# Token-first layout for the turned blocks of u: one 2 KB run per row of each partition-to-partition move

## The chip, the cores and the metric

The kernel runs on one core of a Trainium2 chip. The metric is the device time of one execution in microseconds (us), lower is better. Before the change it is 1478.62 us, the median of 3 runs that lie between 1475.41 and 1482.45.

## The reference

The input `x` has 8 batches of 3136 tokens with 256 features. An FNet mixing (the real part of an FFT over the tokens and over the features) is followed, row by row, by a SoLU block with a layer norm between its two products:

```python
X = np.fft.fft(np.fft.fft(x, axis=1), axis=2).real   # 8 x 3136 x 256
x = X.reshape(25088, 256)
h = x @ w_in                                          # 1024 features
e = np.exp(h - max(h)); sm = e / (sum(e) + 1e-9)
solu = h * sm
ln = (solu - mean(solu)) / sqrt(var(solu) + 1e-6) * g_ln
out = ln @ w_out                                      # 25088 x 256
```

All of it is fp32.

## The kernel before, in words

The batches are taken in 4 pairs. The FFT over 3136 = 49 x 64 tokens is done in two steps: `transform1` works on the 49 and writes its result to DRAM (`zd`), `turn` (L156) reads it back with other axes on the partitions (4 DMAs, L160), and `transform2` (L163) does the 64. The FFT over features is folded into the weights `Wi`. By symmetry one pair needs 25 values of the index `k1`; a **unit** is one pair at one `k1`, so there are 100 units. A unit gives two tiles of 128 tokens by 1024 features, sign 0 and sign 1 (a row and its mirror image); the four units with `k1` = 0 have sign 0 alone.

Within a unit the work goes over the engines like this. TensorE forms the even and the odd half of h (`up`, L195, into two PSUM buffers). VectorE takes the even half (`even`, L201), joins the halves into h for each sign and finds the maximum (`join`, L209, L214). ScalarE takes the exponential (`expo`, L220). VectorE multiplies it by h (`product`, L228), which gives u. ScalarE squares u for the variance (L237), while VectorE turns the same u in blocks of 32 x 32 (`turn_blocks`, L258, and L260 for a unit with one sign). For the second product the features must lie on the partitions. The blocks are turned, but each still sits in the wrong group of 32 partitions, so `move_blocks` (L262) sends each of the 4 x 4 pairs of partition groups to its place with one DMA (L269): 16 DMAs of 64 KB for each unit, all issued by the SP queue. TensorE then multiplies (`down`, L275): 8 chunks of 128 features, with the turned u as the stationary operand (the one that LDWEIGHTS loads) and `Wo` as the moving one. Each fp32 product is two LDWEIGHTS and two MATMUL in the profile, so a unit has 32 of these. `store` (L278) scales the result on ScalarE (L281); sign 0 leaves by two DMAs of SP (L289), sign 1 by an indirect DMA of GpSimd (L284).

The order of the work is written out by hand (L421 to L452), and each engine and queue goes through its own instructions in that order. In the iteration of unit i, TensorE does `up` of i, `transform2` of unit i+1, a piece of `transform1` for the next pair (16 of the 25 iterations, in three of the four pairs), and `down` of unit i-2. SP gets, in order: a store of `transform1` (L154, every second piece) or at one place in each pair the four DMAs of `turn`, then the two stores of unit i-2, the 16 moves of unit i, and a load of the next pair's input (L96). So a unit's turned blocks have somewhat under two iterations to arrive. VectorE also folds the next pair's input (L109 to L111), in 8 of the 25 iterations. Tile `v` has 2 buffers, `uT` 3, the PSUM pool that `down` writes to 4.

Before the change the tile `v` holds, in each partition, feature first and sign innermost: element (f, s) is at 2f + s. A 32 x 32 block is 32 neighbouring f, and a move takes, from each of 32 partitions, 8 separate runs (one for each chunk of 128 features) of 64 numbers, 256 bytes. `uT` holds chunk first, then token and sign, so `down` reads its stationary operand with a step of 2 numbers, 8 bytes.

Of the kernel before, what the change touches and what calls it, by code (L numbers as in the profile page):

```python
# [8 lines left out]
FP32 = mybir.dt.float32  # L9
# [6 lines left out]
P = 128  # L16
# [15 lines left out]
def kernel(  # L32
# [19 lines left out]
    nc = tc.nc  # L52
    B, S, D = x.shape
    FF = moe_w_in.shape[1]
    KF = FF // P
# [21 lines left out]
    Wo = const.tile([P, KF, D], FP32, name="Wo")  # L77
# [29 lines left out]
    def fold_features(o, i):  # L107
        up, down = i[:, :, 1:128], i[:, :, 255:128:-1]
        nc.vector.tensor_tensor(out=o[:, :, 1:128], in0=up, in1=down, op=ALU.add)  # L109
        nc.vector.tensor_tensor(out=o[:, :, 129:256], in0=up, in1=down, op=ALU.subtract)  # L110
        nc.vector.tensor_copy(out=o[:, :, 0:129:128], in_=i[:, :, 0:129:128])  # L111
# [141 lines left out]

    def turn_blocks(t, s):

        if s == 0:
            t.v = fpool.tile([P, FF, 2], FP32, tag="v", name="v32", bufs=2)
        nc.vector.transpose(out=t.v[:, :, s], in_=t.u[s])  # L258
        if len(t.signs) == 1:
            nc.vector.transpose(out=t.v[:, :, 1], in_=t.u[s])  # L260

    def move_blocks(t):  # L262

        t.uT = fpool.tile([P, KF, 4, 64], FP32, tag="uT", name="uT", bufs=3)
        v = t.v.rearrange("p (c q n) s -> p q c (n s)", q=4, n=32)
        for i in range(4):
            for q in range(4):
                a, b = slice(32 * i, 32 * i + 32), slice(32 * q, 32 * q + 32)
                nc.sync.dma_start(out=t.uT[b, :, i, :], in_=v[a, q])  # L269

    def down(t, s):
        uT = t.uT.rearrange("p c i (n s) -> p c (i n) s", s=2)
        ps = ps_m.tile([P, D], FP32, tag="m", name="ps_o")
        for c in range(KF):
            nc.tensor.matmul(ps, uT[:, c, :, s], Wo[:, c, :], start=(c == 0), stop=(c == KF - 1))  # L275
        return ps

    def store(t, s, ps):  # L278
# [124 lines left out]
    with tc.manual_schedule():  # L403
# [13 lines left out]
        fpool = ctx.enter_context(tc.tile_pool(name="fpool", bufs=2))  # L417
# [3 lines left out]
        for i in range(len(units) + 2):  # L421
# [14 lines left out]
            if old:  # L436
                ps_o = [down(old, s) for s in old.signs]
            if cur:
                for s in cur.signs:
                    product(cur, s)  # L440
                for s in cur.signs:
                    square(cur, s)
                    turn_blocks(cur, s)
            if old:
                store(old, 0, ps_o[0])
            if cur:
                move_blocks(cur)
                stats(cur)
# [80 lines left out]
```

## Time and profile before

| | |
|---|---|
| median of 3 runs | 1478.62 us |
| the profiled execution's own time | 1484.27 us |
| its span (first to last instruction) | 1482.5 us |
| mean granted TensorE clock | 0.936 |
| matmul busy | 1223.0 us (82%) |
| VectorE busy | 961.7 us (65%) |
| ScalarE busy | 613.8 us (41%) |
| GpSimd busy | 471.9 us (32%) |
| bytes moved by DMA | 189.66 MB in 486718 packets |

The profile is of one execution. PE is TensorE's matmul, PEld its loading of weights, DVE VectorE, ACT ScalarE, POOL GpSimd, SP the sync engine, which only issues DMAs here; a q behind a name is the engine's instruction queue. A row of the timeline has the start, the duration, the engine, the line, the operation, the tile written and the tiles read, the count, and in brackets the idle time before it and what ended that. A row of a line's instructions has the smallest, median and largest duration in ns and the first and last start in us. A group row has busy time and mean ns. Runs of like instructions are merged into one row of a timeline, so that the difference of two starts gives the pace.

### The profile page before, as it was taken

The numbers are of one execution on the slowest core, as the hardware profiler recorded it, in microseconds if no ns is written. First come the engines' busy times: TensorE is split into PE (matmuls) and PEld (weight loads), VectorE is DVE, ScalarE is ACT, GpSimd is POOL, SyncE is SP. The second block draws the span as 40 slices with busy tenths as digits, with TensorE's granted clock in tenths as the row PEclk, the third lists the DMA queues.
The fourth block names the chain that finished last, engine by engine and source line by source line (L and its number), as shares of the span: only waits on it lengthen the run. The fifth ranks groups of instructions, "written<-read, shape, count | busy, mean of one in ns | idle before, by whom it ended". The sixth has DMA issues, their size and how long they took to land.

```text
span 1482.5 us, 17170 instructions
## 1 busy us (share of the span) xinstructions
PE 1223.0 (82%) x4864; PEld 916.3 (62%) x4864; DVE 961.7 (65%) x1481; ACT 613.8 (41%) x1149; POOL 471.9 (32%) x892
## 2 busy tenths in 40 slices
PE   1633798999959889998959899889968889989996
PEld 1312476667747667676747577657746666767665
DVE  2598766767646676767655676666646666767671
ACT  0101454444534444445434345444524444444441
POOL 3400434343213334434213343333212333333331
PEclk8566999999979999999989999999998999999998
DMA  9540665655574656555574656555574444444443
GB/s 243 178 84 0 139 139 143 149 134 125 124 159 107 139 143 145 134 148 126 118 159 108 146 125 150 139 145 129 116 164 110 108 103 109 109 107 109 108 110 85
DMA packets 486718, 189.66 MB, mean 128 GB/s; under 512 B 446326, under 2 KB 472702, under 8 KB 486368
## 3 DMA queue, kind: packets, MB, share of 16 engines
q1 hardware_dynamic: 471952, 157.61, 48.0%
q0 software_dynamic: 8704, 25.44, 5.9%
q10 hardware_dynamic: 5968, 5.52, 1.7%
q8 instruction: 40, 0.66, 0.2%
q14 instruction: 54, 0.44, 0.1%
HBM read 44.78 MB, written 38.80 MB: 56 GB/s over the span
## 4 chain that ended last, share of the span: by engine, by line
SPq 44%; PE 30%; DMA 13%; DVE 6%; issue 5%; POOL 1%; ACT 1%; POOLq 0%; ACTq 0%; DVEq 0%
SPq L269 39%; PE ps_o L275 19%; PE ps_h L195 9%; SPq L289 4%; DMA uT<-v 4%; DMA g<-zd 3%; DMA xa<-in_x_dram 2%; DMA out_dram<-ot 2%; DVE ex L302 2%; PE ps L169 1%; DMA xb<-in_x_dram,idx 1%; POOL xa L118 1%; PE ps L149 1%; DVE h L209 0%; DVE rest L330 0%
## 5 line engine op out<-in xcount | busy, mean ns | idle before, releaser
L275 PE MATMUL ps_o<-Wo,uT 128*128 128x256 f32 x3136 | 730.7, 393 | 161.9 <-DMA uT<-v 87.2
L275 PEld LDWEIGHTS ps_o<-Wo,uT 128*128 128x128 f32 x3136 | 628.4, 203 | 247.4 <-issue 149.6
L195 PE MATMUL ps_h<-Wi,q 128*128 128x512 f32 x800 | 360.2, 593 | 4.0 <-DVE ev L201 2.5
L228 DVE SCALAR_TENSOR_TENSOR u<-h,u 128x1024 f32<-128x1024 f32 x196 | 232.7, 1224 | 140.6 <-ACT u L220 140.6
L237 ACT ACTIVATE h<-u,nmean 128x1024 f32<-128x1024 f32 x196 | 223.6, 1142 | 229.4 <-POOL nmean L230 229.4
L284 POOL DMA_INDIRECT out_dram<-ot,idx x96 | 114.6, 1194 | 605.1 <-DMA out_dram<-ot 395.2
L220 ACT ACTIVATE u<-h,neg 128x1024 f32<-128x1024 f32 x196 | 223.6, 1141 | 188.0 <-DVE neg L214 186.2
L209 DVE CUSTOM_DVE_ANT_0 h<-ev,ps_h 128x1024 f32<-128x1024 f32 x196 | 231.7, 1219 | 77.9 <-PE ps_h L195 46.9
L201 DVE SCALAR_TENSOR_TENSOR ev<-w_mid,q,ps_h 128x1024 f32<-128x1024 f32 x100 | 127.8, 1278 | 217.6 <-PE ps_h L195 217.3
L195 PEld LDWEIGHTS ps_h<-Wi,q 128*128 128x128 f32 x800 | 151.7, 190 | 152.4 <-issue 145.6
L258 DVE STREAM_TRANSPOSE v<-u 128x1024 f32<-128x1024 f32 x196 | 233.0, 1228 | 0.1
L177 ACT COPY q<-ps 128x257 f32<-128x257 f32 x100 | 37.4, 374 | 253.8 <-PE ps L171 253.7
L230 POOL TENSOR_SCALAR nmean<-usum 128x1 f32<-128x1 f32 x196 | 84.0, 440 | 161.2 <-DVE u L228 159.3
L149 PE MATMUL ps<-y,F 98*100 98x258 f32 (+3 forms) x288 | 80.3, 419 | 41.1 <-DVE y L111 41.0
L281 ACT ACTIVATE ot<-ps_o,rs 128x256 f32<-128x256 f32 x196 | 83.9, 459 | 69.8 <-PE ps_o L275 69.7
L169 PEld LDWEIGHTS ps<-T,g 128*128 128x128 f32 x400 | 60.4, 191 | 47.4 <-issue 47.4
L149 PEld LDWEIGHTS ps<-y,F 98*100 98x100 f32 x288 | 48.0, 191 | 54.7 <-DVE y L111 21.3
L118 POOL TENSOR_TENSOR xa<-xa,xb 98x1020 f32<-98x1020 f32 (+1 forms) x32 | 72.7, 2272 | 27.7 <-DMA xa<-in_x_dram 19.0
L249 POOL TENSOR_SCALAR v<-ssq 128x2 f32<-128x2 f32 (+1 forms) x100 | 25.0, 250 | 169.6 <-ACT h L237 169.6
L252 POOL TENSOR_TENSOR rs<-v,neg_half 128x2 f32<-128x2 f32 (+1 forms) x100 | 72.0, 720 | 7.8
L169 PE MATMUL ps<-T,g 128*128 128x128 f32 x400 | 60.7, 274 | 0.0
L152 ACT COPY z<-ps 100x512 f32<-100x512 f32 x64 | 36.2, 569 | 36.5 <-PE ps L149 27.2
(53 smaller groups left out, 461.0 us busy)
## 6 DMA issues: line engine op xcount, KB each, us to landing
uT<-v SPq DMA_DIRECT2D x1600, 64.0 KB
zd<-z SPq DMA_DIRECT2D x32, 400.0 KB
g<-zd SPq DMA_DIRECT2D x16, 800.0 KB
out_dram<-ot SPq DMA_DIRECT2D x200, 64.0 KB
xa<-in_x_dram SPq DMA_DIRECT2D x32, 392.0 KB
raw_in_moe_w_in_dram<-in_moe_w_in_dram ACTq DMA_DIRECT2D x1, 2048.0 KB
raw_in_moe_w_out_dram<-in_moe_w_out_dram ACTq DMA_DIRECT2D x1, 2048.0 KB
out_dram<-ot,idx POOLq DMA_INDIRECT x96, 2.9
```

Of the source, the lines that this page charges most:

```text
L149: nc.tensor.matmul(o[..., cs], F[:, 2 * t + h, :], i[..., cs], start=first, stop=True, skip_group_check=True)
L169: nc.tensor.matmul(ps[:, h * P : (h + 1) * P], pr.g[:, k1, h * P : (h + 1) * P], T[:, k1, :], start=(h == 0), stop=True, skip_group_check= ...
L195: nc.tensor.matmul(ps[:, fs], t.q[:, c * P : (c + 1) * P], Wi[:, c, fs], start=True, stop=True)
L201: nc.vector.scalar_tensor_tensor(out=t.ev, in0=w_mid, scalar=t.q[:, KD * P :], in1=ps, op0=ALU.mult, op1=ALU.add)
L209: nc.vector.tensor_tensor_reduce(out=t.h[s], in0=t.ev, in1=ps, scale=1.0, scalar=-3.0e38, op0=ALU.subtract if s else ALU.add, op1=ALU.max, ...
L220: nc.scalar.activation(out=t.u[s], in_=t.h[s], func=ACT.Exp, bias=t.neg[:, s : s + 1], accum_out=t.esum[:, s : s + 1])
L228: nc.vector.scalar_tensor_tensor(out=t.u[s], in0=t.h[s], scalar=1.0, in1=t.u[s], op0=ALU.mult, op1=ALU.mult, accum_out=t.usum[:, s : s + 1])
L237: nc.scalar.activation(out=t.h[s], in_=t.u[s], func=ACT.Square, bias=t.nmean[:, s : s + 1], accum_out=t.ssq[:, s : s + 1])
L258: nc.vector.transpose(out=t.v[:, :, s], in_=t.u[s])
L269: nc.sync.dma_start(out=t.uT[b, :, i, :], in_=v[a, q])
L275: nc.tensor.matmul(ps, uT[:, c, :, s], Wo[:, c, :], start=(c == 0), stop=(c == KF - 1))
L284: nc.gpsimd.indirect_dma_start(out=out, out_offset=bass.IndirectOffsetOnAxis(ap=idx[:, i : i + 1], axis=0), in_=ot, in_offset=None)
```

## The change

The axes of `v` and `uT` are put in another order. In each partition `v` is now ordered by group of partitions q, token n within the group, chunk c and sign s: element (q, n, c, s) is at 512q + 16n + 2c + s. The block turn writes in that order, so its neighbouring results lie 16 numbers (64 bytes) apart, where they were 2 numbers (8 bytes) apart. What one move takes from one partition, all n, c and s of one q, is now a single run of 512 numbers (2 KB), in the source as in the destination. `down` reads its stationary operand with a step of 16 numbers. The number of instructions and DMAs on each engine, their bytes, their order and the buffers are as before; the second turn of a unit with one sign is issued from the same line.

```diff
     def turn_blocks(t, s):
 
         if s == 0:
-            t.v = fpool.tile([P, FF, 2], FP32, tag="v", name="v32", bufs=2)
-        nc.vector.transpose(out=t.v[:, :, s], in_=t.u[s])
-        if len(t.signs) == 1:
-            nc.vector.transpose(out=t.v[:, :, 1], in_=t.u[s])
+            t.v = fpool.tile([P, 4, 32, KF, 2], FP32, tag="v", name="v32", bufs=2)
+        u = t.u[s].rearrange("p (c q r) -> p c q r", q=4, r=32)
+        for o in (s,) if len(t.signs) == 2 else (0, 1):
+            nc.vector.transpose(out=t.v[:, :, :, :, o].rearrange("p q n c -> p c q n"), in_=u)
 
     def move_blocks(t):
 
-        t.uT = fpool.tile([P, KF, 4, 64], FP32, tag="uT", name="uT", bufs=3)
-        v = t.v.rearrange("p (c q n) s -> p q c (n s)", q=4, n=32)
+        t.uT = fpool.tile([P, 4, 32, KF, 2], FP32, tag="uT", name="uT", bufs=3)
         for i in range(4):
             for q in range(4):
                 a, b = slice(32 * i, 32 * i + 32), slice(32 * q, 32 * q + 32)
-                nc.sync.dma_start(out=t.uT[b, :, i, :], in_=v[a, q])
+                nc.sync.dma_start(out=t.uT[b, i], in_=t.v[a, q])
 
     def down(t, s):
-        uT = t.uT.rearrange("p c i (n s) -> p c (i n) s", s=2)
+        uT = t.uT.rearrange("p i n c s -> p (i n) c s")
         ps = ps_m.tile([P, D], FP32, tag="m", name="ps_o")
         for c in range(KF):
-            nc.tensor.matmul(ps, uT[:, c, :, s], Wo[:, c, :], start=(c == 0), stop=(c == KF - 1))
+            nc.tensor.matmul(ps, uT[:, :, c, s], Wo[:, c, :], start=(c == 0), stop=(c == KF - 1))
         return ps
```

## The prediction

> **What bounds the kernel now.** I read the page first, then the chain of waits by line, then the queue of SP and TensorE's timeline over the same stretch of the last pair, where nothing is prepared for a next one.
>
> ```profile
> span 1482.5 us, 17170 instructions
> SPq 44%; PE 30%; DMA 13%; DVE 6%; issue 5%; POOL 1%; ACT 1%; POOLq 0%; ACTq 0%; DVEq 0%
> q1 hardware_dynamic: 471952, 157.61, 48.0%
> uT<-v SPq DMA_DIRECT2D x1600, 64.0 KB
> L269 SPq DMA_DIRECT2D uT<-v x1600: 585/609/1978, 148.2 to 1468.2; - x178
> ```
>
> The issuing queue of SP carries more of the chain than any engine, and its work is the moves: 1600 DMAs at a median of 609 ns. 1600 x 256 runs of 256 bytes are 409,600 of the 471,952 packets on its queue.
>
> ```profile
> 1310.16 1.18 SPq L289 DMA_DIRECT2D out_dram<-ot  x2
> 1311.44 11.76 SPq L269 DMA_DIRECT2D uT<-v  x16
> 1323.32 1.18 SPq L289 DMA_DIRECT2D out_dram<-ot  x2
> 1324.61 10.48 SPq L269 DMA_DIRECT2D uT<-v  x16
> 1335.19 1.18 SPq L289 DMA_DIRECT2D out_dram<-ot  x2
> ```
>
> SP issues without a pause: two stores and 16 moves are 11.87 us in the second unit (1323.32 to 1335.19). The row of 11.76 shows that issuing is sometimes held up beyond its 10.48.
>
> ```profile
> 1311.92 7.15 PE L275 MATMUL ps_o<-Wo,uT 128*128 128x256 f32 x32 [0.91 <-DMA out_dram<-ot]
> 1318.91 3.60 PE L195 MATMUL ps_h<-Wi,q 128*128 128x512 f32 x8
> 1322.34 0.61 PE L169 MATMUL ps<-T,g 128*128 128x128 f32 x4
> 1322.79 0.28 PE L171 MATMUL ps<-g,T 128*128 128x1 f32 x2
> 1324.90 8.84 PE L275 MATMUL ps_o<-Wo,uT 128*128 128x256 f32 x32 [1.83 <-DMA uT<-v]
> PE ps_o L275 <- DMA uT<-v: 87.2, 38, 14.4
> PE ps_o L275 <- DMA out_dram<-ot: 50.1, 18, 14.3
> ```
>
> TensorE does a unit in 6.99 + 3.43 + 0.45 + 0.28 = 11.15 us (differences of starts) and then waits for the blocks. Its two waits, 137 us together, both stand ahead of `down`; the landing of a store that is named in the second has nothing to do with `down`, so I read both as the moves.
>
> How long a unit takes on average:
>
> ```profile
> L214 DVE TENSOR_SCALAR neg<-nmax x100: 153/168/946, 142.9 to 1446.9; 128x2 f32<-128x2 f32 x96, 128x1 f32<-128x1 f32 x4
> g<-zd SPq DMA_DIRECT2D x16, 800.0 KB
> 749.36 3.98 SPq L160 DMA_DIRECT2D g<-zd  x4
> 758.65 15.99 SPq L269 DMA_DIRECT2D uT<-v  x16
> 776.47 8.85 PE L275 MATMUL ps_o<-Wo,uT 128*128 128x256 f32 x32 [14.39 <-DMA uT<-v]
> ```
>
> L214 runs once a unit: 1304.0 us over 99 steps. At three places the `turn` of the next pair goes to the queue ahead of the moves, which then take 15.99 us to issue, and TensorE waits 14.39. I take 15 us for each of the three, so an ordinary unit has (1304.0 - 45) / 99 = 12.72 us. That is the number to move.
>
> **The change part by part: SP.** The 16 moves stay; each has 32 runs of 2 KB in place of 256 of 256 bytes. What does an issue cost with fewer runs?
>
> ```profile
> L289 SPq DMA_DIRECT2D out_dram<-ot x200: 467/587/4453, 171.4 to 1475.4; - x100
> L154 SPq DMA_DIRECT2D zd<-z x32: 274/472/531, 25.7 to 1075.9; - x32
> 615.97 0.53 SPq L96 DMA_DIRECT2D xa<-in_x_dram  x1
> ```
>
> A store moves 64 runs of 1 KB and takes 587 ns, the write of z 100 runs of 4 KB and takes 472. So issuing barely follows the number of runs. The ends are 472 and the present 609; a move over 32 partitions is nearest to the store with its 64, so I take 587. With the pause of 10.48 / 16 - 0.609 = 0.046 us, 16 moves are 10.1 us, a gain of 0.35. With the stores and pauses SP has 11.5 us a unit. Preparing the next pair adds 8 writes of z (0.47), 8 loads (0.53), their pauses and the 4 of `turn` (3.98): about 14 us over 25 units, 0.56 a unit in three pairs of four, so 0.42 on average: 11.9. The same sum today is 11.87 + 0.42 = 12.3, and 12.72 was measured: 0.4 us a unit is the holding up seen in the 11.76. With an eighth of the packets I let the cause of that go; the end on the other side is that it stays.
>
> **TensorE.** Its unit is 11.15 us, plus a piece of `transform1` in 48 units of 100:
>
> ```profile
> 710.05 1.09 PE L149 MATMUL ps<-y,F 98*100 98x258 f32 x4
> L275 PEld LDWEIGHTS ps_o<-Wo,uT x3136: 192/196/338, 161.5 to 1477.0; 128*128 128x128 f32 x196
> L195 PEld LDWEIGHTS ps_h<-Wi,q x800: 186/190/190, 137.9 to 1443.3; 128*128 128x128 f32 x160
> ```
>
> That makes 11.15 + 0.52 = 11.7 us. The new step of 64 bytes concerns LDWEIGHTS alone. With 8 bytes it takes 196 ns, against 190 for a contiguous operand in L195. It lies beside the previous matmul: in `down` one pair of the two takes 6.99 / 32 = 218 ns, in L169 (1322.34 to 1322.79) a load and a 128-column matmul pass every 112 ns, so a load needs no more than 112 of the 218 it has. Doubled it is 224, 6 ns over, 0.2 us a unit. I cost it at nothing, with that as the upper end while the loads still overlap; the rival below is the case where they don't.
>
> **VectorE.** The two turns of a unit now write with a step of 64 bytes. No large VectorE operation here has such a step; the only rows are the tiny copies of two numbers from each token, 512 bytes apart:
>
> ```profile
> L111 DVE COPY y<-xa x32: 158/169/2765, 18.5 to 1046.8; 98x8 f32<-98x8 f32 x32
> L111 DVE COPY y<-x x4: 151/158/159, 63.5 to 1047.3; 98x2 f32<-98x2 f32 x4
> L258 DVE STREAM_TRANSPOSE v<-u x196: 1184/1239/1308, 145.7 to 1451.9; 128x1024 f32<-128x1024 f32 x196
> 1310.58 1.22 DVE L209 CUSTOM_DVE_ANT_0 h<-ev,ps_h 128x1024 f32<-128x1024 f32 x1 [0.53 <-PE ps_h L195]
> 1316.89 2.37 DVE L258 STREAM_TRANSPOSE v<-u 128x1024 f32<-128x1024 f32 x2
> 1320.83 1.28 DVE L201 SCALAR_TENSOR_TENSOR ev<-w_mid,q,ps_h 128x1024 f32<-128x1024 f32 x1 [1.57 <-PE ps_h L195]
> L110 DVE TENSOR_TENSOR y<-xa x32: 660/678/696, 17.9 to 1046.2; 98x508 f32<-98x508 f32 x32
> ```
>
> Six more elements cost 11 ns between the medians (7 between the minima): 1.8 ns each (1.2). A turn now takes 2.37 / 2 = 1.19 us, 1.16 ns an element with everything in it. At 1.8 ns it would be about 1.9 us, plus a little start: I take 2.0, 0.8 more. The ends are 1.19 (nothing) and 2.4 (doubled).
>
> The Trainium skill, on the page "SBUF — State Buffer" (section "Door 1: The DMA port swizzle"), speaks against the change here: a line of this memory is 16 bytes, and an access pattern that does not hit each line at least twice pays a penalty, for which it gives no number. The step of 8 bytes has two hits, that of 64 has one; L258 and L111 agree with the rule as far as so few elements can.
>
> What covers the 0.8: VectorE's loop over a unit is 8.68 us from the first join (1310.58) to the end of the turns (1319.26), and 1.28 for `even`, 9.9 in all, waits for ScalarE included. The 1.57 us before `even` is its wait for TensorE. Folding (two passes of 0.68 and the copy, 1.5 us in 8 of 25 units, three pairs) adds 0.4. So VectorE goes from 10.3 to 11.9 us, under today's 12.72 but level with SP (11.9) and TensorE (11.7). The end of the turns moves back 1.6 us, and SP's moves behind them; the blocks have nearly two iterations, so that alone delays nothing.
>
> **The sum.** Today the unit lies 0.4 us over its largest resource. With three level ones I take the same again: 11.9 + 0.4 = 12.3 us, 0.42 less than now, 42 us over 99 units. The three `turn` stalls stay, as 4 x 800 KB still go ahead of the moves. At the end SP no longer lags behind the last turns: 4 us. The profiled execution would go from 1484.27 to 1438; it is 5.65 above the median of the runs, so the forecast is **1433 us**.
>
> **The rivals.**
> *Faster still.* The turns cost nothing more and an issue drops to 472 ns. SP is then at 10.1, VectorE at 10.3, TensorE's 11.7 binds, and with 0.35 above it a unit has 12.05: 66 us and 4, median 1409. For it: minima of L111 only 7 ns apart. Against: the stores' 587.
> *The turns double.* VectorE has 9.9 + 2.4 + 0.4 = 12.7 us, and binds alone; with 0.1 to 0.4 above it 12.8 to 13.1, 8 to 38 us more, less 4 at the end: median 1483 to 1513, middle 1498. It decides from turns of about 2.2 us. For it: the 1.8 ns may be too low for long rows. The rule on lines would end here if one hit costs two cycles.
> *The loads of weights become the bound.* If a load does not overlap and pays what a contiguous one does not (190 + 112 = 302 ns for a pair), `down` has 32 x 302 = 9.7 us, TensorE 14.35 us, 1.63 over today: 161 us more, and the run is 1636. It decides from about 250 ns, where TensorE passes 12.7. Against it: the 112 ns above.
> *No change.* The packets were not what held SP, and an issue costs 609 ns whatever it carries: 12.72 stays, 1475 to 1479. The Trainium skill, "DMA: Bandwidth & Descriptors" (section "Why small descriptors are slow (HBM only)"), has transfers within SBUF free of the penalty on small ones, which would leave the bytes as slow as now. For it: 587 beside 609. Against it: 10.48 and 11.76 for the same DMAs.
>
> **How the numbers follow.** Forecast 0.42, faster still 0.23, turns double 0.15, loads 0.1, no change 0.1. A change of under 0.5% can't be told from none in this kernel. So faster 0.65, same 0.12 (no change, and the low edge of the doubled turns), slower 0.23. The range goes from TensorE's bound with hardly a wait (11.9 us a unit, 1395) to past the doubled turns (1515); the loads' case is left out. The likeliest case alone has 1410 to 1460.
>
> **What would show it.** Right: the moves' queue pauses between units; packets fall by some 358,000 (1600 x 224); L258 near 2.0 us; the 137 us of waits ahead of `down` fall to about 60, nearly all at the three `turn` places; LDWEIGHTS of L275 may be longer while 32 matmuls still take 7.0 us. Wrong: L269 at 609 ns and still without a pause; L258 above 2.2 us with VectorE never idle before `even`; or 32 matmuls of `down` in over 8 us at full clock.

## The result, and the profile after

The changed kernel takes 1437.72 us, the median of 4 runs, against 1480.12 for the kernel before on the same chip: a ratio of 0.972, with a 95% interval of 0.968 to 0.975. The forecast was 1433. The profiled execution took 1439.91 us.

The page of the changed kernel: its span, the DMA queue that SP feeds, the chain's shares, and the turn among the costliest groups (the change adds a line, so the moves are L270, the turns L262, `down` L276):

```profile
span 1438.1 us, 17170 instructions
DMA packets 128318, 189.66 MB, mean 132 GB/s; under 512 B 36726, under 2 KB 63102, under 8 KB 127968
q1 hardware_dynamic: 113552, 157.61, 43.6%
PE 53%; SPq 24%; DMA 9%; DVE 8%; issue 4%; ACT 1%; POOL 1%; POOLq 0%; DVEq 0%; ACTq 0%
L262 DVE STREAM_TRANSPOSE v<-u 128x1024 f32<-128x1024 f32 x200 | 369.7, 1921 | 0.1
```

The instructions of three lines (least, median and longest ns, then the first and the last start in us): the moves, the loads of weights of `down`, and the tiny step on VectorE whose first and last rows count the units:

```profile
L270 SPq DMA_DIRECT2D uT<-v x1600: 507/589/1832, 148.9 to 1422.1; - x178
L276 PEld LDWEIGHTS ps_o<-Wo,uT x3136: 291/307/338, 161.0 to 1432.7; 128*128 128x128 f32 x196
L214 DVE TENSOR_SCALAR neg<-nmax x100: 153/170/705, 142.4 to 1402.4; 128x2 f32<-128x2 f32 x96, 128x1 f32<-128x1 f32 x4
```

And the longest of its waits on TensorE (us in total, times, longest):

```profile
PE ps_o L276 <- DMA uT<-v: 79.5, 25, 13.5
```

The packets fell by 358,400, but the DMA engines' share only from 48.0% to 43.6%, which is 712 and 627 us of each engine's time over the two spans: most of it goes with the bytes. A move's issue fell from 609 ns to 589. Both long steps cost time: a turn has 1921 ns in place of 1228, a load of weights 307 in place of 196. L214 gives 1260.0 us over 99 units where it gave 1304.0, and this difference of 44 us is the whole gain.

The chain now names TensorE first; the first experiment shows that this misleads. The timeline of SP over a stretch of the last pair (begin, duration, instructions):

```profile
1271.59 11.29 SPq L270 DMA_DIRECT2D uT<-v  x16
1282.98 1.17 SPq L290 DMA_DIRECT2D out_dram<-ot  x2
1284.26 10.05 SPq L270 DMA_DIRECT2D uT<-v  x16
1294.41 1.17 SPq L290 DMA_DIRECT2D out_dram<-ot  x2
1295.69 10.06 SPq L270 DMA_DIRECT2D uT<-v  x16
```

The timeline of TensorE over the same stretch:

```profile
1284.45 7.44 PE L276 MATMUL ps_o<-Wo,uT 128*128 128x256 f32 x32 [1.05 <-DMA uT<-v]
1291.72 3.60 PE L195 MATMUL ps_h<-Wi,q 128*128 128x512 f32 x8
1295.16 0.61 PE L169 MATMUL ps<-T,g 128*128 128x128 f32 x4
1295.60 0.28 PE L171 MATMUL ps<-g,T 128*128 128x1 f32 x2
```

SP still issues with hardly a pause (its waits for ScalarE ahead of the stores, L290, are 19.6 us in the whole run, 6.8 before); 16 moves go out in 10.05 us in place of 10.48, and now and then one is still held up (the 11.29). TensorE waits for blocks less often, but it waits: 79.5 us ahead of `down`, three of them at `turn`, 13.3 to 13.5 each.

### The profile page after: what moved, and what is told of

Read it like the earlier page. It is cut to its first block, busy times and chain, and to the rows that moved or that the text cites. A ratio compares the mean times of both kernels' runs of the same rounds, so it can differ in the third digit from the quotient of the medians.

```text
span 1438.1 us, 17170 instructions
## 1 busy us (share of the span) xinstructions
PE 1239.2 (86%) x4864; PEld 996.2 (69%) x4864; DVE 1084.9 (75%) x1481; ACT 611.9 (43%) x1149; POOL 482.8 (34%) x892
## 3 DMA queue, kind: packets, MB, share of 16 engines
q1 hardware_dynamic: 113552, 157.61, 43.6%
## 4 chain that ended last, share of the span: by engine, by line
PE 53%; SPq 24%; DMA 9%; DVE 8%; issue 4%; ACT 1%; POOL 1%; POOLq 0%; DVEq 0%; ACTq 0%
PE ps_o L276 33%; SPq L270 21%; PE ps_h L195 15%; DMA g<-zd 3%; DMA uT<-v 3%; PE ps L149 2%; SPq L290 2%; PE ps L169 2%; DMA xa<-in_x_dram 2%; DVE ex L303 2%; DVE h L209 1%; DVE v L262 1%; DMA xb<-in_x_dram,idx 1%; DVE y L111 1%; DMA out_dram<-ot 1%
## 5 line engine op out<-in xcount | busy, mean ns | idle before, releaser
L276 PE MATMUL ps_o<-Wo,uT 128*128 128x256 f32 x3136 | 750.3, 399 | 92.8 <-DMA uT<-v 79.5
L276 PEld LDWEIGHTS ps_o<-Wo,uT 128*128 128x128 f32 x3136 | 717.0, 307 | 116.2 <-issue 95.2
L262 DVE STREAM_TRANSPOSE v<-u 128x1024 f32<-128x1024 f32 x200 | 369.7, 1921 | 0.1
L230 POOL TENSOR_SCALAR nmean<-usum 128x1 f32<-128x1 f32 x196 | 94.8, 492 | 229.0 <-DVE u L228 227.6
L109 DVE TENSOR_TENSOR y<-xa 98x508 f32<-98x508 f32 x32 | 21.4, 669 | 39.1 <-POOL xa L118 34.8
```

The source lines that it names most:

```text
L262: nc.vector.transpose(out=t.v[:, :, :, :, o].rearrange("p q n c -> p c q n"), in_=u)
L276: nc.tensor.matmul(ps, uT[:, :, c, s], Wo[:, c, :], start=(c == 0), stop=(c == KF - 1))
```

## The experiments

Twelve kernels ran, four to twelve times each, beside the kernel before, whose median in these groups of runs was 1483.5 to 1486.7.

**First question: are the three resources level, as the prediction's sum has it, or does one bind alone?** Four kernels take the parts of the change apart. The prediction's theory: SP, TensorE and VectorE are level, so taking the steps away brings a little. The rival: the steps stand on the path.

The runs alone. The turn writes into the old order and `down` reads with the old step, while a move still copies 2 KB in one run; the numbers of u come out in mixed places.

```diff
-            nc.vector.transpose(out=t.v[:, :, :, :, o].rearrange("p q n c -> p c q n"), in_=u)
+            nc.vector.transpose(out=t.v.rearrange("p q n c s -> p (q n c s)").rearrange("p (c q n s) -> p c q n s", q=4, n=32, s=2)[:, :, :, :, o], in_=u)
...
-        uT = t.uT.rearrange("p i n c s -> p (i n) c s")
+        uT = t.uT.rearrange("p i n c s -> p (i n c s)").rearrange("p (c x s) -> p x c s", x=P, s=2)
```

> The moves keep their runs of 2 KB, but the turn writes and the loads of weights read with the old step of 8 bytes (the numbers of u come out in mixed places; what is computed from them is not the reference's). Theory of three level resources: the turn is back at 1.2 us and LDWEIGHTS at 196 ns, so VectorE has 10.3 us and TensorE 11.7 a unit, but SP keeps its 11.9 and still issues without a pause; a unit goes from 12.3 to 12.1, and the time to about 1420. Rival (the steps stand on the path with all they cost): 1.5 us of VectorE and 0.3 of TensorE come off a unit until TensorE's 11.7 binds, and the time is about 1395 or less. Rival (only the step counted, the runs nothing): faster than before by nothing, 1480.

Measured 1437.79 us, ratio 0.969 (0.9665 to 0.9714): the changed kernel's own time. The turn and `even` among its costliest groups:

```profile
L262 DVE STREAM_TRANSPOSE v<-u 128x1024 f32<-128x1024 f32 x200 | 237.1, 1224 | 1.3 <-DVE u L228 0.6 <-DMA out_dram<-ot 0.4
L201 DVE SCALAR_TENSOR_TENSOR ev<-w_mid,q,ps_h 128x1024 f32<-128x1024 f32 x100 | 127.8, 1278 | 160.2 <-PE ps_h L195 160.0 <-DVE Wo L378 0.2
```

Its loads of weights, by line, and below them SP's timeline:

```profile
L276 PEld LDWEIGHTS ps_o<-Wo,uT x3136: 192/196/338, 154.3 to 1430.8; 128*128 128x128 f32 x196
```

```profile
1236.45 1.17 SPq L290 DMA_DIRECT2D out_dram<-ot  x2
1237.72 10.86 SPq L270 DMA_DIRECT2D uT<-v  x16
1248.69 1.17 SPq L290 DMA_DIRECT2D out_dram<-ot  x2
1249.97 10.05 SPq L270 DMA_DIRECT2D uT<-v  x16
```

The turns and loads are as cheap as before the change, and VectorE merely waits longer ahead of `even` (160 us, where the changed kernel has 64). SP's rows are the same. So removing all that the steps cost gained nothing: SP binds alone. All three forecasts are wrong, that of the three level resources least.

The steps alone. The changed kernel's turns and loads, but each move is cut into 8 runs of 256 bytes (the numbers are mixed again).

```diff
+        v = t.v.rearrange("p q n c s -> p (q n c s)").rearrange("p (c q x) -> p q c x", q=4, x=64)
+        uT = t.uT.rearrange("p i n c s -> p (i n c s)").rearrange("p (c i x) -> p c i x", i=4, x=64)
...
-                nc.sync.dma_start(out=t.uT[b, i], in_=t.v[a, q])
+                nc.sync.dma_start(out=uT[b, :, i, :], in_=v[a, q])
```

> The steps of 64 bytes stay in the turn and in the loads of weights, but the moves are cut into 8 runs of 256 bytes as before (again the numbers are mixed up). Theory of three level resources: SP is again the largest with 12.3 us and its hold-ups, VectorE (11.8) and TensorE (11.95) stay under it, and the steps cost only by the end of the turns coming 1.3 us later: 1480 to 1495, no slower than before by more than 1%. Rival (the steps on the path): 1.5 us more a unit, 1600 or more.

Measured 1485.13 us, ratio 1.0008 (0.9990 to 1.0026): the steps cost nothing that can be measured while SP binds, and the runs are the whole gain. The theory of level resources expected this time too, so it is the runs alone that speak against it.

One step alone. From the changed kernel, only `down`'s line edited as in the runs alone, or only the turn's (numbers mixed in both).

> Runs of 2 KB, the turn with the step of 64 bytes, the loads of weights with 8 (numbers mixed up). The turn stays at 1.85 to 1.92 us, LDWEIGHTS is at 196 ns, 32 matmuls of down take 6.99 us in place of 7.27. Theory of three level resources: 0.27 us off one of three, so at most 10 us faster than the changed kernel: 1427 to 1437. Rival (TensorE alone binds after the change): 0.27 us of every unit, 27 us, 1410.

> Runs of 2 KB, the turn with the step of 8 bytes, the loads of weights with 64 (numbers mixed up). LDWEIGHTS stays at 307 ns, the turn is at 1.2 us. Theory of three level resources: VectorE drops to 10.3, TensorE with 11.95 and SP with 11.9 are left: 1425 to 1437. Rival (VectorE alone binds after the change): 1.3 us off, bound then by TensorE: 1405.

Measured 1437.04 us, ratio 0.9688 (0.9665 to 0.9710), and 1442.54, 0.9708 (0.9682 to 0.9735). Neither differs from the change itself by more than the noise; neither step was a bound.

**Second question: what in SP's issuing costs, the count of issues or the packets?** First the other direction: 128-byte runs, from the kernel before, with the sign outermost.

```diff
-            t.v = fpool.tile([P, FF, 2], FP32, tag="v", name="v32", bufs=2)
-        nc.vector.transpose(out=t.v[:, :, s], in_=t.u[s])
+            t.v = fpool.tile([P, 2, FF], FP32, tag="v", name="v32", bufs=2)
+        nc.vector.transpose(out=t.v[:, s, :], in_=t.u[s])
...
-        v = t.v.rearrange("p (c q n) s -> p q c (n s)", q=4, n=32)
+        v = t.v.rearrange("p s (c q n) -> p q (s c) n", q=4, n=32)
...
-            nc.tensor.matmul(ps, uT[:, c, :, s], Wo[:, c, :], start=(c == 0), stop=(c == KF - 1))
+            nc.tensor.matmul(ps, uT[:, s * KF + c, :], Wo[:, c, :], start=(c == 0), stop=(c == KF - 1))
```

> From the kernel before, with the sign outermost in v and uT: a move has 16 runs of 128 bytes from each partition, 512 in place of 256, the turn writes and the loads read without a step. Theory (an issue has a fixed part and a small one by the number of runs, 20 ns for the 224 runs that the change took away): about 632 ns a move, 0.37 us more a unit, and 1515. Rival (issuing does not depend on runs, the 20 ns come from the count of dimensions): 609 ns and 1480. Rival (packets in flight bind): the DMA engines' time for the moves nearly doubles, and the time passes 1600.

Measured 1526.50 us, ratio 1.027 (1.0243 to 1.0298). Its DMA queue on the page, then its moves and its loads of weights:

```profile
q1 hardware_dynamic: 881552, 157.61, 61.7%
```

```profile
L269 SPq DMA_DIRECT2D uT<-v x1600: 585/632/3224, 149.9 to 1510.3; - x178
L275 PEld LDWEIGHTS ps_o<-Wo,uT x3136: 186/190/338, 164.4 to 1521.0; 128*128 128x128 f32 x196
```

The median issue is the expected 632 ns. So 32, 256 and 512 runs a move give 589, 609 and 632 ns: mostly a fixed price. The last 23 ns are 37 us over 1600 moves and the time rose by 40. The DMA engines now fill 61.7%, and still the issue accounts for the time.

Then fewer issues with the same packets. From the kernel before, 8 of a unit's 16 moves are put together into two DMAs over all 128 partitions (their numbers stay in their own partitions and so in the wrong place).

```diff
-        for i in range(4):
+        for i in range(2, 4):
+            nc.sync.dma_start(out=t.uT[:, :, i, :], in_=v[:, i])
+        for i in range(2):
             for q in range(4):
```

> The kernel before with its runs of 256 bytes, all on SP's queue, but 8 of a unit's 16 moves put together into two DMAs over all 128 partitions (each piece stays in its own partition, so these numbers reach the wrong place): 10 issues in place of 16, the same bytes and the same 409,600 packets, no second queue and so no wait between queues. Theory (the count of issues on SP binds): 6 x 0.65 us less, SP at about 8.5 us a unit, TensorE binds as in the run with short steps, runs of 2 KB and 4 moves on ScalarE's queue: 1330 to 1350. Rival (small packets bind, and the issue only mirrors them): SP's row is held up as long as before, 1450 or more. Between: a DMA of 1024 packets takes some 0.2 us longer to issue than one of 256, 0.4 us a unit, all of it still covered.

Measured 1325.68 us, ratio 0.893 (0.890 to 0.895), the lowest time of all, with the runs of 256 bytes. Its DMA queue on the page, the two kinds of moves by line, SP's timeline and TensorE's:

```profile
q1 hardware_dynamic: 462352, 157.57, 53.3%
```

```profile
L267 SPq DMA_DIRECT2D uT<-v x200: 659/671/3840, 147.0 to 1302.5; - x100
L271 SPq DMA_DIRECT2D uT<-v x800: 585/616/4487, 148.5 to 1308.3; - x160
```

```profile
1213.94 1.39 SPq L267 DMA_DIRECT2D uT<-v  x2
1215.37 5.72 SPq L271 DMA_DIRECT2D uT<-v  x8
1223.41 1.17 SPq L291 DMA_DIRECT2D out_dram<-ot  x2
```

```profile
1203.40 7.16 PE L277 MATMUL ps_o<-Wo,uT 128*128 128x256 f32 x32
1210.39 3.60 PE L195 MATMUL ps_h<-Wi,q 128*128 128x512 f32 x8
1213.83 0.61 PE L169 MATMUL ps<-T,g 128*128 128x128 f32 x4
1214.27 0.28 PE L171 MATMUL ps<-g,T 128*128 128x1 f32 x2
1214.41 7.16 PE L277 MATMUL ps_o<-Wo,uT 128*128 128x256 f32 x32
```

A DMA of 256 KB and 1024 packets is issued in 671 ns, hardly more than one of 64 KB. SP has finished its moves at 1221.09 and pauses until 1223.41; TensorE goes through a unit in 11.01 us (1203.40 to 1214.41) with no gap. The packets themselves leave no queue behind: by the packet records of the traces, the last packet of a unit's moves ends 1.2 us (median over the units) after SP has issued the last of them in the kernel before, 1.1 in the changed kernel, 1.2 here, and 1.3 with runs of 128 bytes. And the moves' packets take a DMA engine 485 us on average here and 489 in the kernel before, so putting moves together did not make the transfers cheaper. This settles it: the count of issues was the bound of the kernel before, and small packets at this rate are not one.

**Third question: what do the steps cost once SP is relieved?** Four of the 16 moves go to ScalarE's queue, in the changed kernel and in the kernel with the runs alone.

```diff
-                nc.sync.dma_start(out=t.uT[b, i], in_=t.v[a, q])
+                (nc.scalar if i == 3 else nc.sync).dma_start(out=t.uT[b, i], in_=t.v[a, q])
```

> The changed kernel, with 4 of a unit's 16 moves (those out of partitions 96 to 127) issued from ScalarE's queue and 12 from SP's. Theory after the first four runs (SP's issuing alone binds, each with its 0.63 us): SP has 2.5 us less a unit, 9.4, and TensorE with its longer loads (11.95) and VectorE with its longer turns (11.8) bind next: a unit goes from 12.27 to about 12.05, the time to 1410 to 1420. Rival (the bytes or the packets in flight bind, whoever issues): no change, 1437.

> As the run with the runs of 2 KB and both steps back at 8 bytes (numbers mixed up), with 4 of the 16 moves issued from ScalarE's queue. Theory (SP's issuing alone binds): SP at 9.4 lets TensorE bind with 11.7, VectorE has 10.3: a unit takes 11.8 to 11.9, the time 1390 to 1400, so that the steps cost 15 to 25 us once SP is relieved. Rival (bytes in flight bind): 1437.

Measured 1373.74 us, ratio 0.925 (0.922 to 0.928), and 1336.63, 0.900 (0.897 to 0.902; numbers mixed). TensorE's timeline in the changed kernel with the split, then SP's:

```profile
1203.90 7.44 PE L276 MATMUL ps_o<-Wo,uT 128*128 128x256 f32 x32
1211.18 3.60 PE L195 MATMUL ps_h<-Wi,q 128*128 128x512 f32 x8
1214.61 0.61 PE L169 MATMUL ps<-T,g 128*128 128x128 f32 x4
1215.06 0.28 PE L171 MATMUL ps<-g,T 128*128 128x1 f32 x2
1215.20 7.44 PE L276 MATMUL ps_o<-Wo,uT 128*128 128x256 f32 x32
```

```profile
1204.03 7.52 SPq L270 DMA_DIRECT2D uT<-v  x12
1214.03 1.14 SPq L290 DMA_DIRECT2D out_dram<-ot  x2
```

SP pauses 2.5 us (1211.55 to 1214.03), and TensorE goes without a gap, 11.30 us a unit. Both times are some 40 to 60 us under what I expected, in part because I had put TensorE at 11.95 us with its piece of `transform1`, where these rows give 11.30 + 0.52 = 11.8, and had allowed for waits that these rows don't show. The steps cost 37 us here: 11.30 against 11.0 us of TensorE in each unit is 28 of them; the other 9 are not traced to a place.

The same split of the kernel before was to show its packets with a relieved SP. I tried it with the moves out of partitions 96 to 127, then, because the pieces of two queues interleaved there, with those into partitions 96 to 127.

```diff
-                nc.sync.dma_start(out=t.uT[b, :, i, :], in_=v[a, q])
+                (nc.scalar if q == 3 else nc.sync).dma_start(out=t.uT[b, :, i, :], in_=v[a, q])
```

> The kernel before, runs of 256 bytes and steps of 8, with 4 of the 16 moves issued from ScalarE's queue; nothing else is changed. Theory (SP's issuing alone binds): SP has 12.3 - 2.6 = 9.7 us, TensorE's 11.7 binds, and the time is 1390 to 1405: faster than the changed kernel with the same split, since the turns and the loads have no long step. Rival (the number of packets counts by itself, with 409,600 still to be moved): 1450 or more.

> The kernel before with 4 of the 16 moves issued from ScalarE's queue, now those into partitions 96 to 127: in the first split of this kernel the moves of the two queues wrote interleaved pieces of the same partitions, SP waited 365 us for moves of the other queue, and the run says nothing on issuing. Theory (SP's issuing alone binds): without those waits SP has 9.7 us a unit, TensorE binds as in the run with runs of 2 KB, short steps and the same number of moves on ScalarE's queue (1337), and the time is 1335 to 1355, faster than the changed kernel with 4 moves on ScalarE's queue (1374) by the price of its steps. Rival (409,600 small packets bind once two queues issue them): 1400 or more.

Measured 1589.01 us, ratio 1.071 (1.068 to 1.074), and 1591.64, 1.072 (1.067 to 1.076). Both got slower. The second kernel's waits of SP's queue, two rows of its timeline, and two of ScalarE's queue between them; last, the same waits in the changed kernel with the split:

```profile
SPq L269 <- DMA uT<-v: 375.6, 110, 6.2
```

```profile
1211.18 14.12 SPq L269 DMA_DIRECT2D uT<-v  x12
1226.69 10.28 SPq L269 DMA_DIRECT2D uT<-v  x12
```

```profile
1221.11 0.59 ACTq L269 DMA_DIRECT2D uT<-v  x1
1221.74 1.95 ACTq L269 DMA_DIRECT2D uT<-v  x3
```

```profile
SPq L270 <- DMA uT<-v: 70.5, 70, 4.4
```

Twelve moves should take 7.9 us and take 14.12, since SP waits 375.6 us for landings of other moves; the changed kernel with the split has 70.5 of these. My reason (interleaved pieces) is wrong, as the second split has none and waits as long. The trace shows what it waits for. The moves of both queues tell of their landing by the same eight semaphores (counters that instructions wait on), and a move waits until the one that used its semaphore before it has landed. Of the 375.6 us, 370.5 end with the landing of a move that ScalarE's queue issued. In the row of 14.12, SP stands still from 1217.08 until 1223.25, when the move that ScalarE issued at 1221.11 has landed; that one belongs to the next unit and had itself waited for the next unit's turn on VectorE, which ended at 1221.09. So SP's moves of one unit wait for work of the next, and nearly all waits of this kernel are of that kind. In the changed kernel with the split SP waits for ScalarE's moves too (69.8 of the 70.5 us), but mostly for those of the same unit. Why the semaphores are handed out in one order with runs of 256 bytes and in another with 2 KB is open. Neither run says what the packets cost; the run with 10 issues does.

Last, `turn`'s four DMAs one in each of four iterations, in the changed kernel with the split and in the kernel before with it.

```diff
-        elif step - 4 == NH // 2:
-            turn(pr)
+        elif NH // 2 <= step - 4 < NH // 2 + 4:
+            turn(pr, step - 4 - NH // 2)
```

> The changed kernel with 4 of the 16 moves on ScalarE's queue and the four DMAs of turn issued in four iterations, one in each. Theory (the three stalls of 10 us at turn come from 3.2 MB put ahead of a unit's moves at once; 800 KB at a time fit in the slack that the moves have): the stalls go, 20 to 30 us off the 1374 of the split alone: 1345 to 1355. Rival (the same bytes delay the same moves, spread or not): 1374.

> The kernel before, steps of 8 bytes and runs of 256, with 4 of the 16 moves (into partitions 96 to 127) on ScalarE's queue and turn in four iterations. Theory: with SP relieved TensorE binds with 11.0 us a unit and the pieces of transform1, nothing waits at turn, 1310 to 1325. Rival (small packets bind): 1390 or more, and the layout with runs of 2 KB is the better one also with two queues.

Measured 1375.88 us, ratio 0.925 (0.924 to 0.927), and 1585.17, 1.066 (1.061 to 1.071). The first gains nothing; the second still has SP's waits between the queues and tells nothing of `turn`. In the first, the moves of the four iterations around the spread DMAs are held up instead of one unit's:

```profile
376.48 8.45 SPq L271 DMA_DIRECT2D uT<-v  x12
384.97 0.59 SPq L161 DMA_DIRECT2D g<-zd  x1
389.01 13.32 SPq L271 DMA_DIRECT2D uT<-v  x12
404.35 10.73 SPq L271 DMA_DIRECT2D uT<-v  x12
417.07 11.86 SPq L271 DMA_DIRECT2D uT<-v  x12
```

By its time the rival held: spreading gains nothing. But SP's waits for landings of moves rose as well, from 70.5 to 109.2 us, so the run doesn't separate the bytes' share from theirs. The fastest kernel that still computes the reference is the changed one with 4 moves on ScalarE's queue, 1373.74 us.

## Why the prediction was right, point by point

**What bounds the kernel.** Right: SP's issuing queue. The run with 10 issues shows it: the same packets, 160 us less.

**SP's term.** Right in size: 587 ns expected, 589 measured, 16 moves in 10.05 us for 10.1. That is 0.43 us a unit less between the rows of 10.48 and 10.05, and 0.43 x 99 is 43 of the 44 us. But the step "with an eighth of the packets I let the cause of that go" failed. About as much as before remains over the sum: an ordinary unit has (1260.0 - 45) / 99 = 12.27 us, and SP's bare sum, taken as before with the stores and their pauses (10.05 + 1.17 + 0.2) and 0.42 for the next pair, is 11.8 to 11.9. So 0.4 us still lies above it. Between the first and the last L214, what the moves' issues take beyond their median fell from 39 to 18 us in the trace, but SP's pauses of over 0.3 us grew from 23 to 36 us, and long issues of the stores stayed (34 and 31 us beyond the median); what holds a single issue up is open.

**The sum.** The step "with three level ones I take the same again" failed too: there are no three level ones. The runs alone and the steps alone show SP alone as the bound, both before and after. I took 0.4 us off for hold-ups that didn't go as a whole, and put 0.4 on for a crowding that isn't there. The two errors cancel by luck, and 12.3 a unit came out for 12.27 measured. The 4 us put down for the end did not come: from the last L214 to the end of the span both kernels take about 35.6 us (1446.9 to 1482.5 and 1402.4 to 1438.1). The forecast is nearer than its reasons deserve.

**VectorE.** The turn was put at 2.0 us between 1.19 and 2.4, and has 1.92; the row of eight-number copies was a fair guide. It was covered, more fully than I thought.

**TensorE.** The loads of weights were given 224 ns a pair as their upper end; 32 matmuls of `down` take 7.27 us (1284.45 to 1291.72), 227 ns a pair, 0.28 us a unit over the old 6.99. Slightly over my end, and hidden. (The 11.15 us of a unit count its last 0.28 whole; without gaps a unit takes 11.01, as the run with 10 issues shows.) A load has 1.57 times its old duration (307 and 196 ns), the turn 1.56 times (1921 and 1228), neither double. The rule of the Trainium skill on SBUF lines (page "SBUF — State Buffer", section "Door 1: The DMA port swizzle"), a penalty below two hits for each line of 16 bytes, agrees with this trace. In the run with 128-byte runs, which has no step at all, a load takes 190 ns and a turn 1234 (medians), so the step of 8 bytes costs next to nothing; no run has a step between 8 and 64 bytes, so none shows where the cost begins.

**The stalls at `turn`.** They stayed, as forecast. The 137 us of waits ahead of `down` fell to 84 (79.5, and 4.1 put down to a store), not to 60, for SP still hardly paused. That sign, "the moves' queue pauses between units", was wrong, and the run with the runs alone gives the reason. So was the sign of 7.0 us for 32 matmuls, which take 7.27.

**The rivals.** The doubled turns and the loads as the bound both failed on their prices. "No change" failed on the 20 ns an issue. Its premise, that transfers within SBUF pay no penalty for small packets, is not what the runs show: the moves' packets, with the same bytes, take a DMA engine 717, 489 and 409 us on average with 128 bytes, 256 bytes and 2 KB; but the engines were not the bound. "Faster still" failed on the stores' 587 ns, as I argued; cheap turns alone would not have brought it, for the run with the runs alone has them and gains nothing by them.

## What to carry to other kernels

When a queue issues without a pause, add up its issues before anything else: here a DMA costs 0.6 us to issue whether it has 32 runs or 512, so fewer DMAs are worth more than better ones (160 us against 42, though the kernel with 10 issues leaves numbers in the wrong place and shows only the price). A cost that is well below the bound shows nothing in the time until the bound is moved, so price it in the kernel in which it would bind: the long steps cost 0 us here and 37 with a second queue. And when several resources look level, take one away in an experiment before adding an allowance for crowding.

## What the runs showed of the hardware that was not expected

- An issue on SP takes 589, 609 and 632 ns for 32, 256 and 512 runs over 32 partitions, and 671 for 1024 runs over 128 partitions (median of each).
- Eight times fewer packets for the same bytes brought the DMA engines' share of this queue from 48.0% to 43.6% only; halving the runs to 128 bytes brought it to 61.7%. In all three the last packet of a unit's moves ended 1.1 to 1.3 us (median over the units) after the last issue.
- A step of 64 bytes takes a load of weights from 196 to 307 ns and a block turn's writes from 1228 to 1921 ns.
- Moves on two queues that share completion semaphores can wait for each other: SP waits 375.6 us for landings of moves, 370.5 of them for moves of ScalarE's queue, with runs of 256 bytes, and 70.5 with the same number of moves split off and runs of 2 KB.
